# A recurrent layer with a routed expert layer: fixed slots for two chunks instead of one, the upper halves of four chunks moved between engines, and a new set of ranks

## The chip, the cores and the metric

The kernel runs on one core of a Trainium2 chip. The metric is device time in microseconds from the start to the end of one execution; several executions are timed and their median is given. The engines are named as the profile names them: PE (TensorE matmuls) and PEld (its weight loads), DVE (VectorE), ACT (ScalarE), POOL (GpSimd) and SP (SyncE, which here only issues transfers).

## The reference, cut to what matters

```python
# x, r_gate, i_gate: (4, 5056, 256); a_param: (256,)
a_base = 1 / (1 + exp(-a_param))
a_t    = exp(8 * sigmoid(r_gate) * log(clip(a_base)))
x_g    = sqrt(max(1 - a_t * a_t, 1e-6)) * sigmoid(i_gate) * x
h      = a_t[:, t] * h + x_g[:, t]        # a scan over 5056 steps, y[:, t] = h
# the 4 * 5056 = 20224 rows of y go through 8 experts, one for each row
e_idx  = argmax(y @ w_gate)               # the row's expert
gate_w = softmax(y @ w_gate)[e_idx]
eom    = sigmoid(y @ w_output_gate)[e_idx]
out    = gate_w * eom * (relu(y @ w1[e_idx]) @ w2[e_idx])   # w1: 256 x 1024, w2: 1024 x 256
```

## The kernel before, in words

The 20224 tokens are 158 tiles of 128, worked off in 20 chunks of 8 tiles (the last has 6). `chunk(c)` is the front of the kernel. It loads the three inputs in two blocks of 512 tokens, forms the decay and the gated input on ACT and DVE (L570 to L592), scans on DVE (L623), finds a power of two that scales the block (`top`, `norm`, `scale_`), and splits the scaled state into two fp16 parts: `hi`, the upper half (L676 on ACT, or L678, a tensor_scalar on DVE, by the letter of the chunk in `UPPERS`), and `lo`, what is left (L681, DVE). `project` (L702, PE) transposes each tile's two halves and forms the gate logits; `row` (L709, ACT) copies the tile's rows to `rows_all`, and `lz` (L713, DVE) sums the logits. Then come the choice of the expert, the token's rank within it (`ranks`, L743 and L745, PE), its weight and its position, and 8 indirect transfers on POOL (`scatter_rows`, L391) that write the rows of the chunk into the DRAM buffer `xs`, sorted by expert.

The expert weights are loaded in fp32 and split into two fp16 parts that stay in SBUF (`w1r`, `w2r`). `unit(u, ...)` does this for one of 16 matrices (unit 2e is w1 of expert e, unit 2e+1 its w2): a load (L451), a small Gram product on PE that gives a scale (`gram`, L477), then `hi` (L510, ACT) and `lo` (L524, DVE). A unit's fp32 data is staged where the split unit two further on will stand; the last two units, 14 and 15, are staged in the ring `ws`.

Tokens meet their experts in two ways. `slot(s)` takes a number of rows (128 or 256, at the end 64) of one expert, which is only known on the chip: it loads the rows transposed (L1047), copies the expert's w1 from `w1r` to a tile `ws` (two transfers, L1063), multiplies (L1091), takes relu on ACT (L1106) and the lower half on DVE (L1111), multiplies by w2 out of `w2r` (L1137), scales (L1150) and stores rows by an indirect transfer (L1153). `turn(c, e)` is a fixed slot: expert e's first 128 tokens of chunk c have 128 rows of their own in `xs`, so that the expert is known when the program is written and w1 and w2 are read where they lie, with no `ws` copy (L908, L930, L946, L973 or L980, L994, L997). In the turns of chunk 0 with e under 7, called raw, the second product is done in fp32 with the staged, unsplit w2 (L973); the other turns use the split w2 (L980), and DVE forms the lower half of h (L949). Rows of turns that no token fills come from a filling of zeros (`fill`, L1193). Tokens beyond the 128 of a fixed slot go to the ordinary slots.

Which chunk has how many slots is settled when the program is written. Before: 8 turns in chunk 0; 5 slots of 128 in chunk 1, 8 in chunk 2; then 62 slots of 256, three or four in a chunk and one in chunk 3; at the end 23 slots of 128 and 8 of 64. The last 9 and 4 of these stand behind a branch that is taken only if a token needs them (`SPARE`, `THIN_SPARE`, `unused`).

The order of work on every engine is fixed when the program is written, by `in_order`: a list scheduler with estimated times, in which each piece of work has a rank (`UNIT_RANK`, `CHUNK_RANK`, `ROUND_RANK`, `SLOT_RANK`, `UNIT_LOAD` and others) and the lowest rank among the ready ones goes first. Buffers are rings (`Ring`): a tile waits until the tile n before it is released, and until its predecessor in the ring has begun. A ring's order is the order in which the calls stand in the program, so that the place of the call matters:

```python
scaled += [unit(u, STAGED.get(u)) for u in range(E, 2 * E - 2)]   # units 8 to 13
for e in range(HOLD if ROUNDS else 0):
    turn(0, e)
...                                                              # then units 14 and 15
if c < ROUNDS:
    for e in range(0 if c else HOLD, E):
        turn(c, e)
```

The ring `ps_h` (3 tiles) is shared by the units' Gram products and by the first product of the turns and slots.

Of the kernel before, what the change touches and what calls it, by code (L numbers as in the profile page):

```python
# [25 lines left out]
SIZES = (8, 8)  # L26
WIDTHS = (128,128,128)
MODES = 'SSSSSSSSSSSSSSSS'
ROUNDS = 1
HOLD = 0  # L30
RAW = 7
TURNS = (870,)
RESERVE = {128:500,256:1100}
GROW = 80

SPLITS = {"S": "ACT", "D": "DVE"}
SCALED = {"ACT": 1.02, "DVE": 0.7}
SQUARES = 'AAAAA'
UPPERS = 'AAAAA'
BOUNDS = 'AAAAAAAADDDDDDDDDDDD'  # L40

RT = 2
# [6 lines left out]
LANDING = {"Pool": 2.0, "SP": 0.5}  # L49
ADDRESS = 1.11  # L50
SWITCH = 1.28
LAG = 0.00115
ALONE = (0, 1, 2, 3, 4, 5, 6, 7)
QUICK = -11.74482
ROOT = 872.46984
EARLY = -3356.52202
UNIT_RANK = (14.784, 1.135, 649.126, 1304.642, -3219.631, -118.358, 953.446, -19.714, 619.598, 551.943, 729.966, -184.356, 791.67, 1318.467, -195.084, 200.882)
CHUNK_RANK = (-8.611, 721.162, 1331.441, 1446.348, 941.149, 843.802)
FILL = 154.31313
ROUND_RANK = (-265.341,)  # L60
TURN = 103.07338
SLOT_RANK = (837.564, 517.995, 614.48, 621.619)
LOAD_RANK = 5.18213
STAGED = {14: ('ws', 'ws'), 15: ('ws', 'ws')}
WINDOW, WARM = 3.413, (0.8, 0.35)
UNIT_LOAD = (39.858, 449.082, 537.194, 43.57, -91.278, 168.502, 435.996, 1305.65, 173.591, -125.648, -166.337, -60.891, 955.38, -3351.625, 57.178, 964.301)
CHUNK_LOAD = (7.699, -0.953, -160.403, 959.152, 155.261, -58.702)
TAIL = -3981.4538
TOPS = 2
TABLES = -188.10427  # L70
DEPTH = 3
SLACK = (0.152, 0.728, 0.933, 1.2, 0.778, 0.203)
PACE = 9.85e-05

SPREAD = (2.0, 2.6)

SPARE = 9
THIN = 64
HOMES = ("rt", "it", "xt", "ws", "rt", "it", "xt", "ws", "ws")
THIN_AT = 12  # L80
# [112 lines left out]
def rglru_moe(ctx: ExitStack, tc: tile.TileContext, x, r_gate, i_gate, a_param, wg, wog, w1, w2, out, shape):  # L193
# [26 lines left out]
    for c, (t, n) in enumerate(chunks):  # L220
        pending += n * P
        bound_left += n * P
        if c < ROUNDS:
            pending -= TURNS[c]
            bound_left -= min(P, bound_left)
# [21 lines left out]

    xs = tc.dram_tile([E * REGION + ROUNDS * E * P + VOID, ROW // 2], F32, name="xs")

# [117 lines left out]
    zrow = const.tile([P, ROW], F16, name="zrow")  # L367
    dummy = E * REGION + ROUNDS * E * P
    last_row = dummy + VOID
# [20 lines left out]
    def scatter_rows(pos, rows, c):  # L390
# [3 lines left out]
        ins = op.ins  # L394
        past = [tiles["fill"]] if c < ROUNDS else []
        tc.declare_no_dep(ins, group="xs", keep=past, reason="rows of xs are written once, ahead of the loads that read them")
# [144 lines left out]
    def chunk(c):  # L541
# [66 lines left out]
        for b, nb, m, g0, key, ru, iu, xu, root, inputs, scale in blocks:  # L608
            w = work("ACT", 1.04 * scale, root, squares[b // 4:b // 4 + 1] if c in ALONE else squares, rank + ROOT, "S", uses=[iu])
            w = work("DVE", 0.07 + 1.07 * scale, inputs, [w], rank, uses=[iu, xu])  # L610
# [31 lines left out]
        for b in range(0, nt, 4):  # L642
# [30 lines left out]

            def hi(H=H, halves=halves, s_of=s_of, by=UPPERS[c] if c < len(UPPERS) else "A"):
                if by == "A":
# [10 lines left out]
            pu, pold = rings["ps_t"].new()  # L686
            w = work("PE", 0.15, norm, [w, pold], EARLY + c / 100, uses=[pu, au], slack=SLACK[2 + (c > 3)])
            w = work("DVE", 0.33, scale_, [w] + chain["small"], front, uses=[pu])
            by = "DVE" if c < len(UPPERS) and UPPERS[c] == "D" else "ACT"
            w = work(by, (0.1 + 0.95 * scale, 0.07 + 0.7 * scale)[by == "DVE"], hi, [w], front, uses=[iu, xu])  # L690
            cut = work("DVE", 0.07 + 1.15 * scale, lo, [w], front, uses=[iu, xu])
            for j in range(b, b + nb):
# [21 lines left out]

                w = work("PE", 0.277, project, [cut, pold, gates], EARLY + c / 100, uses=[pu, xu], slack=SLACK[c > 3])
                copied.append(work("ACT", 0.48, row, [w, old], front, uses=[pu, used]))
# [57 lines left out]
        def positions():  # L774
# [5 lines left out]

            if c < ROUNDS:
                nc.vector.scalar_tensor_tensor(beyond, carry, -float(P + c * E * P), fixed, op0=ALU.add, op1=ALU.subtract)
# [10 lines left out]
        def counts():  # L793
            pk = tiles["pk", c]
            held = pk[:, nt * E:(nt + 1) * E]
            if c < ROUNDS:
                nc.vector.tensor_scalar(beyond, held, -float(P), 0.0, op0=ALU.add, op1=ALU.max)
                held = beyond
            nc.vector.tensor_tensor(carry, carry, held, op=ALU.add)

        quick = rank + QUICK
        ch = work("DVE", 0.5, choose, lows, quick)
        ex = work("ACT", 0.42, chances, [ch], quick, "E")
        cn = work("DVE", 0.9, chosen, [ch, ex], quick)
        pu, pold = rings["ps_t"].new()
        pk = work("PE", 0.24, ranks, [cn, pold], EARLY + c / 100, uses=[pu], slack=SLACK[c > 3])
        sm = work("DVE", 0.6, sums, [cn, ex], quick)
# [86 lines left out]
    def turn(c, e):  # L894
# [73 lines left out]
        for f in range(NF):  # L968
# [15 lines left out]

            m = work("PE", 0.44 if raw else 0.327, multiply2, [m, evac[f // 4]] + (loaded if raw else split)[2 * e + 1], rank + LAG + f * PACE, uses=[pu, hus[f // 4][0]], slack=SLACK[4] if f == 0 else 0.0)

# [35 lines left out]
    def slot(s):  # L1022
# [103 lines left out]
        for f in range(NF):  # L1126
# [14 lines left out]

            m = work("PE", 0.327 * q, multiply2, [m, evac[f // per], ready] + (every if f == 0 else []), rank + LAG + f * PACE, uses=[pu, hus[f // 4][0], vuse], slack=SLACK[4 + (c > 3)] if f == 0 else 0.0)
            m.placed = True
# [72 lines left out]
    for h in range(2):  # L1216
# [7 lines left out]
        if h == 0:  # L1224
            scaled += [unit(u, STAGED.get(u)) for u in range(E, 2 * E - 2)]
            for e in range(HOLD if ROUNDS else 0):
                turn(0, e)
# [4 lines left out]
    for c in range(NC):  # L1232
# [3 lines left out]
# [3 lines that stand above are left out]
# [59 lines left out]
```

## Time and profile before

| | |
|---|---|
| median of 3 executions | 1034.86 us (1034.28 to 1034.92) |
| the profiled execution: its own time | 1036.0 us |
| its span, first to last instruction | 1034.3 us |
| PE, ACT, DVE, POOL busy, share of the span | 93%, 70%, 66%, 35% |
| mean granted TensorE clock, share of full speed | 0.975 |
| moved by DMA | 245.28 MB |

A busy PE is one with a matmul under way; matmuls overlap, so the mean duration of one is longer than the step from one to the next. The idle time in a row of a group is that of the engine just before the group's instructions.

### The profile page before, as it was taken

To read this page: it belongs to the slowest core of one execution; us is meant where nothing else is said; L and a number is where in the kernel's file an instruction comes from. 1 tells how busy PE (TensorE), PEld (TensorE's weight loads), DVE (VectorE), ACT (ScalarE), POOL (GpSimd) and SP (SyncE) were. 2 spreads that over 40 slices of the span, in tenths; PEclk is the share of its full clock that TensorE was granted. 3 is DMA by queue.
4 is the path that set the end of the run, shared out by engine and by line. 5 is a ranking of instruction groups with operands and counts; after the bars stand their busy time and mean duration, and the time that the engine had idled before them with its cause. 6 is when DMAs were issued, how large, how long until landed. Compare 5 with 4: busy or idle time off the path is not lost.

```text
span 1034.3 us, 29541 instructions
## 1 busy us (share of the span) xinstructions
PE 966.7 (93%) x9884; PEld 869.0 (84%) x9884; DVE 686.4 (66%) x1696; ACT 719.7 (70%) x1149; POOL 360.8 (35%) x346
## 2 busy tenths in 40 slices
PE   3567989889999999999999999999999999999997
PEld 2557978778889888889998999999899888899986
DVE  6696786787777776767677686777867676232231
ACT  8889889989897858677685867768577653232232
POOL 0032361543435342524324243443424234422111
PEclk9857999999999999999999999999999999999999
DMA  9995659998898879777786968778686749636871
GB/s 327 378 362 153 176 167 309 289 317 263 240 267 239 268 213 262 216 231 237 225 241 226 270 228 230 247 210 265 220 250 220 224 155 304 200 115 222 262 226 30
DMA packets 196862, 245.28 MB, mean 237 GB/s; under 512 B 119262, under 2 KB 130527, under 8 KB 196720
## 3 DMA queue, kind: packets, MB, share of 16 engines
q1 hardware_dynamic: 180992, 200.18, 65.3%
q0 software_dynamic: 15728, 43.17, 12.7%
q8 instruction: 94, 1.54, 0.6%
q14 instruction: 48, 0.39, 0.1%
HBM read 79.09 MB, written 45.97 MB: 121 GB/s over the span
## 4 chain that ended last, share of the span: by engine, by line
PE 60%; issue 10%; ACT 10%; DMA 8%; DVE 6%; SPq 3%; POOL 3%; POOLq 0%; ACTq 0%; DVEq 0%
PE po L1137 27%; PE ph L1091 26%; PE pt L702 3%; DMA w2r<-in_moe_w_dram 2%; POOL out_dram L1153 2%; ACT rows_all L709 2%; DVE it L623 2%; PE ph_t L930 1%; DMA ws<-w1r 1%; PE po_t L973 1%; ACT h L1106 1%; DMA it<-in_i_gate_dram 1%; SPq L451 1%; DMA w1r<-in_moe_w_dram 1%; ACT rt L580 1%
## 5 line engine op out<-in xcount | busy, mean ns | idle before, releaser
L1137 PE MATMUL po<-w2r,h 128*128 x3720 | 501.8, 272 | 4.2 <-ACT ot L1150 2.7
L1091 PE MATMUL ph<-xt,ws 128*128 128x256 f16 (+2 forms) x4464 | 494.9, 254 | 7.3 <-DMA ws<-w1r 7.0
L1091 PEld LDWEIGHTS <-ws 128*128 128x128 f16 x4464 | 379.7, 98 | 45.1 <-DMA ws<-w1r 8.7
L1137 PEld LDWEIGHTS <-h 128*128 128x128 f16 x3720 | 355.2, 98 | 48.2 <-issue 5.3
L1106 ACT ACTIVATE h<-ph 128x512 f16<-128x512 f32 (+1 forms) x310 | 182.0, 590 | 229.3 <-PE ph L1091 222.7
L1111 DVE SCALAR_TENSOR_TENSOR h<-ph,h 128x512 f16<-128x512 f32 (+1 forms) x310 | 209.0, 679 | 170.3 <-ACT h L1106 169.3
L1153 POOL DMA_INDIRECT out_dram<-ot,mt x155 | 161.7, 1043 | 399.9 <-ACT ot L1150 365.1
L391 POOL DMA_INDIRECT xs<-rows_all,posi x158 | 178.2, 1128 | 235.9 <-issue 102.7
L709 ACT ACTIVATE rows_all<-pt 128x512 f16<-128x512 f32 x158 | 91.4, 595 | 9.8 <-PE pt L702 5.1
L623 DVE TENSOR_TENSOR_SCAN it<-rt,last,it 128x512 f32<-128x512 f32 (+4 forms) x78 | 96.2, 1241 | 0.3
L1150 ACT ACTIVATE ot<-po,osc 128x256 f32<-128x256 f32 (+1 forms) x155 | 67.5, 472 | 30.5 <-PE po L1137 23.0
L702 PE MATMUL pt<-iw,xt 128*128 128x160 f16 x632 | 71.7, 241 | 13.0 <-ACT xt L676 4.2
L713 DVE TENSOR_REDUCE lz<-pt 128x16 f32<-128x64 f32 x158 | 34.4, 222 | 62.8 <-PE pt L702 37.4
L702 PEld LDWEIGHTS <-xt 128*128 128x128 f16 x632 | 54.2, 102 | 19.3 <-issue 7.1
L592 DVE SCALAR_TENSOR_TENSOR it<-it,xt 128x1024 f32<-128x1024 f32 (+1 forms) x40 | 48.2, 1206 | 29.2 <-ACT it L589 29.2
L580 ACT ACTIVATE rt<-rt,lam 128x512 f32<-128x512 f32 (+1 forms) x80 | 62.0, 812 | 0.2
L681 DVE SCALAR_TENSOR_TENSOR xt<-it,sc,xt 128x1024 f16<-128x1024 f32 (+1 forms) x40 | 50.7, 1267 | 17.2 <-ACT xt L676 17.2
L676 ACT ACTIVATE xt<-it,sc 128x1024 f16<-128x1024 f32 (+1 forms) x40 | 45.6, 1141 | 6.3 <-DVE sc L302 5.1
L576 DVE SCALAR_TENSOR_TENSOR xt<-it,xt 128x1024 f32<-128x1024 f32 (+1 forms) x40 | 48.2, 1205 | 2.5 <-DMA xt<-in_x_dram 1.5
L584 ACT ACTIVATE it<-rt 128x1024 f32<-128x1024 f32 (+1 forms) x40 | 41.8, 1044 | 6.3 <-DVE xt L576 5.8
L589 ACT ACTIVATE it<-it,quarter 128x1024 f32<-128x1024 f32 (+1 forms) x40 | 45.4, 1135 | 0.4
L570 ACT ACTIVATE rt<-rt 128x1024 f32<-128x1024 f32 (+1 forms) x40 | 42.0, 1050 | 3.7 <-DMA rt<-in_r_gate_dram 3.5
(159 smaller groups left out, 702.6 us busy)
## 6 DMA issues: line engine op xcount, KB each, us to landing
ws<-w1r SPq DMA_DIRECT2D x186, 512.0 KB
rt<-in_r_gate_dram SPq DMA_DIRECT2D x39, 512.0 KB
it<-in_i_gate_dram SPq DMA_DIRECT2D x39, 512.0 KB
xt<-in_x_dram SPq DMA_DIRECT2D x39, 512.0 KB
w1r<-in_moe_w_dram SPq DMA_DIRECT2D x7, 1024.0 KB
w2r<-in_moe_w_dram SPq DMA_DIRECT2D x7, 1024.0 KB
xs<-rows_all,posi POOLq DMA_INDIRECT x158, 4.0
out_dram<-ot,mt POOLq DMA_INDIRECT x155, 3.9
```

The source lines that it names most:

```text
L391: op = nc.gpsimd.indirect_dma_start(out=xs[:, :], out_offset=bass.IndirectOffsetOnAxis(ap=pos, axis=0), in_=rows.bitcast(F32), in_offset=None,
L580: nc.scalar.activation(r[:, h], r[:, h], AF.Exp, scale=lam[:, h:h + 1], bias=lam[:, h:h + 1])
L623: nc.vector.tensor_tensor_scan(H[:, h, lo:hi], A[:, h, lo:hi], H[:, h, lo:hi], first, op0=ALU.mult, op1=ALU.add)
L681: nc.vector.scalar_tensor_tensor(halves()[:, 1], H(), s_of(), halves()[:, 0], op0=ALU.mult, op1=ALU.subtract)
L702: nc.tensor.matmul(pt[:, k, h * P:h * P + PIECE], lhsT=halves()[:, k, h, (j % 4) * P:(j % 4 + 1) * P], rhs=iw[:, h, :], start=h == 0, stop ...
L709: nc.scalar.activation(rows_all[:, row_at[j], 0:META].rearrange("p (k h d) -> p k h d", k=2, h=ND), src, AF.Copy)
L1091: nc.tensor.matmul(ph[:, i], lhsT=ws[:, f // 2 % 2, a, c, f % 2 * P:(f % 2 + 1) * P], rhs=xt[:, b * ND + c, 0:w], start=k == 0, stop=k == ...
L1106: newest["relu"] = nc.scalar.activation(part(0, f0), tiles["ph", s, f0], AF.Relu).ins
L1111: nc.vector.scalar_tensor_tensor(part(1, f0), tiles["ph", s, f0], 0.0, part(0, f0), op0=ALU.max, op1=ALU.subtract)
L1137: nc.tensor.matmul(po[:, j], lhsT=hh[:, a, f % 4, j * P:j * P + P], rhs=w2r[:, bass.ds(eo + (b * NF + f) * D, D)], start=f + j + a + b == ...
L1150: nc.scalar.activation(ot[0:pw], tiles["po", s][0:pw, j], AF.Copy, scale=tiles["osc", s][0:pw, j, :])
L1153: op = nc.gpsimd.indirect_dma_start(out=out[:, :], out_offset=bass.IndirectOffsetOnAxis(ap=tiles["mt", s][0:pw, j, 1:2].bitcast(I32), axis=0),
```

## The change

Chunk 1 gets eight fixed slots as chunk 0 has them (`ROUNDS` 2; `TURNS`, the number of tokens that are expected to find room in them), with 1024 more rows in `xs`, which the filling covers as well. By the same rules the slots of 128 become none in chunk 1 and 6 in chunk 2; there are still 62 of 256 (one more in chunks 6 and 9, one less in 7 and 10), and at the end 29 of 128 and 8 of 64, of which the last 15 and 4 stand behind the branch. The fixed slots of chunk 1 are not raw. The turns of experts 0 and 1 of chunk 0 are called ahead of units 14 and 15 (`HOLD` 2), which puts them ahead in the rings. The upper halves of chunks 1 to 4 are formed by DVE (L678) instead of ACT (L676). All ranks and the slacks of the scheduler are new.

```diff
-ROUNDS = 1
-HOLD = 0
+ROUNDS = 2
+HOLD = 2
 RAW = 7
-TURNS = (870,)
+TURNS = (870,870)
...
-UPPERS = 'AAAAA'
+UPPERS = 'ADDDD'
...
-LAG = 0.00115
+LAG = 0.00106
...
-QUICK = -11.74482
-ROOT = 872.46984
-EARLY = -3356.52202
-UNIT_RANK = (14.784, 1.135, 649.126, 1304.642, -3219.631, -118.358, 953.446, ...
-CHUNK_RANK = (-8.611, 721.162, 1331.441, 1446.348, 941.149, 843.802)
-FILL = 154.31313
-ROUND_RANK = (-265.341,)
-TURN = 103.07338
+QUICK = 117.35396
+ROOT = 217.25543
+EARLY = -1051.66239
+UNIT_RANK = (-84.779, 27.039, 146.56, 431.971, 155.352, -58.55, -84.794, ...
+CHUNK_RANK = (-235.93, -111.945, 140.773, 290.077, 20.451, -24.26)
+FILL = 23.029
+ROUND_RANK = (-383.116, -583.193)
+TURN = 5.93459
...
-SPARE = 9
+SPARE = 15
```

Likewise new are `SLOT_RANK`, `LOAD_RANK`, `UNIT_LOAD`, `CHUNK_LOAD`, `TAIL`, `TABLES`, `SLACK` and `PACE`.

## Rows read from the trace of the kernel before

**Rows 1.** The page: busy time by engine, and the span in 40 slices.
```profile
PE 966.7 (93%) x9884; PEld 869.0 (84%) x9884; DVE 686.4 (66%) x1696; ACT 719.7 (70%) x1149; POOL 360.8 (35%) x346
...
PE   3567989889999999999999999999999999999997
...
ACT  8889889989897858677685867768577653232232
```
**Rows 2.** Busy time by stretch: us, PE, PEld, DVE, ACT, POOL, PEclk, DMA share, GB/s.
```profile
0.00:75.00 75.00, 38.93 (x322) 34.69 (x323) 57.56 (x152) 63.77 (x100) 11.30 (x25) 0.80 1.04 363
75.00:90.00 15.00, 7.17 (x58) 6.18 (x56) 9.23 (x27) 14.94 (x23) 0.00 (x0) 0.61 0.75 184
90.00:290.00 200.00, 184.84 (x2095) 166.29 (x2092) 150.28 (x358) 181.41 (x270) 80.90 (x67) 0.99 0.84 243
290.00:1000.00 710.00, 707.89 (x7054) 636.92 (x7052) 461.77 (x1145) 451.16 (x744) 261.94 (x248) 1.00 0.77 232
1000.00:1034.30 34.30, 27.82 (x367) 24.93 (x364) 7.52 (x17) 8.38 (x16) 6.62 (x7) 0.95 0.26 69
```
**Rows 3.** The chain of work that ended last: start, us, what.
```profile
290.60 1.31 PE po L1137 x12
```
**Rows 4.** Waits of PE from 90 to 290 us: total us, times, longest.
```profile
PE ph L1091 <- DMA ws<-w1r: 7.0, 8, 1.9
PE po_t L980 <- ACT ot_t L994: 3.8, 1, 3.8
```
**Rows 5.** Timeline of PE: start, us, what.
```profile
87.50 1.91 PE L477 MATMUL pg<-fw 128*128 128x128 bf16 x16
89.21 3.72 PE L930 MATMUL ph_t<-xt_t,w1r 128*128 128x128 f16 x36
...
951.48 1.17 PE L1091 MATMUL ph<-xt,ws 128*128 128x128 f16 x18
...
956.91 1.17 PE L1091 MATMUL ph<-xt,ws 128*128 128x128 f16 x18
```
**Rows 6.** Busy time by stretch again, two stretches.
```profile
72.00:89.20 17.20, 9.06 (x70) 8.07 (x71) 11.75 (x30) 16.75 (x25) 0.00 (x0) 0.60 0.86 211
...
152.00:290.00 138.00, 127.40 (x1487) 114.48 (x1485) 100.67 (x252) 125.81 (x193) 51.66 (x45) 1.00 0.98 284
```
**Rows 7.** Timelines of POOL and SP: the last scatter of a chunk, its first fetch.
```profile
62.73 0.96 POOL L391 DMA_INDIRECT xs<-rows_all,posi  x1 [0.30 <-issue]
...
68.79 2.27 SPq L908 DMA_TRANSPOSE xt_t<-xs  x1
...
277.44 0.96 POOL L391 DMA_INDIRECT xs<-rows_all,posi  x1 [1.05 <-ACT h L1106]
...
286.13 1.33 SPq L1047 DMA_TRANSPOSE xt<-xs  x1
```
**Rows 8.** Groups of ACT from 90 to 290 us: busy us, mean ns, idle before.
```profile
L1106 ACT ACTIVATE h<-ph 128x512 f16<-128x512 f32 x45 | 26.1, 594 | 2.9 <-PE ph L1091 2.8
...
L589 ACT ACT_TABLE_LOAD x9 | 11.5, 1283 | 0.2
L676 ACT ACTIVATE xt<-it,sc 128x1024 f16<-128x1024 f32 x10 | 11.4, 1145 | 1.7 <-DVE sc L302 1.7
...
L1150 ACT ACTIVATE ot<-po,osc 128x256 f32<-128x256 f32 x19 | 8.6, 469 | 0.5 <-PE po L1137 0.5
```
**Rows 9.** Groups of DVE by shape: busy us, mean ns, idle before.
```profile
L660 DVE TENSOR_REDUCE am<-it 128x1 f32<-128x1024 f32 x23 | 27.8, 1211 | 0.0
...
L383 DVE MEMSET zrow<- 128x264 uint32 x1 | 0.3, 278 | 0.0
```
**Rows 10.** Transfers by line: count, size of one; and the group of the slots' stores.
```profile
ws<-w1r SPq DMA_DIRECT2D x186, 512.0 KB
...
xs<-zrow SPq DMA_DIRECT2D x1, 1056.0 KB
...
L1153 POOL DMA_INDIRECT out_dram<-ot,mt x155 | 161.7, 1043 | 399.9 <-ACT ot L1150 365.1
```

More of the change, by code (lines that the diff above doesn't have):

```diff
@@ L51 @@
 SWITCH = 1.28
-LAG = 0.00115
+LAG = 0.00106
 ALONE = (0, 1, 2, 3, 4, 5, 6, 7)
-QUICK = -11.74482
-ROOT = 872.46984
-EARLY = -3356.52202
-UNIT_RANK = (14.784, 1.135, 649.126, 1304.642, -3219.631, -118.358, 953.446, -19.714, 619.598, 551.943, 729.966, -184.356, 791.67, 1318.467, -195.084, 200.882)
-CHUNK_RANK = (-8.611, 721.162, 1331.441, 1446.348, 941.149, 843.802)
-FILL = 154.31313
-ROUND_RANK = (-265.341,)
-TURN = 103.07338
-SLOT_RANK = (837.564, 517.995, 614.48, 621.619)
-LOAD_RANK = 5.18213
+QUICK = 117.35396
+ROOT = 217.25543
+EARLY = -1051.66239
+UNIT_RANK = (-84.779, 27.039, 146.56, 431.971, 155.352, -58.55, -84.794, 14.651, -43.617, 17.787, -235.287, 145.715, 4.342, -0.395, -798.819, -0.903)
+CHUNK_RANK = (-235.93, -111.945, 140.773, 290.077, 20.451, -24.26)
+FILL = 23.029
+ROUND_RANK = (-383.116, -583.193)
+TURN = 5.93459
+SLOT_RANK = (103.546, 160.443, -183.654, -48.334)
+LOAD_RANK = 39.7946
 STAGED = {14: ('ws', 'ws'), 15: ('ws', 'ws')}
 WINDOW, WARM = 3.413, (0.8, 0.35)
-UNIT_LOAD = (39.858, 449.082, 537.194, 43.57, -91.278, 168.502, 435.996, 1305.65, 173.591, -125.648, -166.337, -60.891, 955.38, -3351.625, 57.178, 964.301)
-CHUNK_LOAD = (7.699, -0.953, -160.403, 959.152, 155.261, -58.702)
-TAIL = -3981.4538
+UNIT_LOAD = (343.79, 237.254, 197.318, 198.135, 397.366, -101.845, -43.231, 105.079, 197.907, 8.526, -185.281, 225.229, 97.674, -117.131, 398.254, 205.512)
+CHUNK_LOAD = (101.047, 25.577, 4.303, 1.54, -185.995, -16.184)
+TAIL = -950.62491
 TOPS = 2
-TABLES = -188.10427
+TABLES = 453.62907
 DEPTH = 3
-SLACK = (0.152, 0.728, 0.933, 1.2, 0.778, 0.203)
-PACE = 9.85e-05
+SLACK = (0.455, 0.656, 0.555, 1.414, 0.584, 0.178)
+PACE = 9.03e-05
 SPREAD = (2.0, 2.6)
-SPARE = 9
+SPARE = 15
 THIN = 64
```

## The prediction

> **What bounds the kernel now.** I read the page first. PE is busy 93% of the span, but the slices say where the missing 7% lie: PE's digits are 3 to 9 in the first nine slices of 25.9 us and 9 from there to the last but one, while ACT stands at 8 or 9 through the first twelve slices and mostly at 5 to 8 after them [rows 1]. So the kernel has two regimes. The table by stretch puts numbers on them: PE is idle 36.1 us of the first 75, 7.8 us of the next 15, 15.2 us from 90 to 290, 2.1 us in the 710 us after that, and 6.5 us in the last 34 [rows 2]. The sum is 67.6 us, the 1034.3 us of the span less PE's 966.7. The chain of waits says the same in another way: by 290 us it is, and from there on stays, an almost unbroken sequence of PE's two products, 12 matmuls in 1.31 us [rows 3]. From there on the end is fixed by how much matmul work is left. What can be won is idle PE time ahead of 290 us, less any work that is added to PE.
>
> Ahead of 290 us three things meet. To 75 us the transfers are full (share 1.04 of 16 engines, 363 GB/s): 16 weight matrices and the inputs of two chunks [rows 2]. From 75 to 90 us PE waits for the front. From 90 to 290 us ACT is busy 181.4 of 200 us, DVE 150.3, and the transfers of the second part of it are full again, 0.98 from 152 to 290 us [rows 2, 6]. Chunk 5, the first whose slots find PE saturated, shows that the front sets the pace: its last scatter starts at 277.4 us and its first fetch at 286.1 us, as soon as the scatter has landed [rows 7].
>
> **The change, part by part.**
>
> *One more slot's work on PE.* Eight fixed slots are added and seven slots of 128 go (13 become 6). The 62 slots of 256 stay. At the end 23 less 9 and 29 less 15 are both 14 slots of 128 ahead of the branch, and 4 of 64. Before, the stores of the slots are 155 [rows 10]: 62 times 2, 13, 14 and 4, so the branch was not taken. Whether it is taken after, I counted from the reference's own inputs: the fixed slots take 871 tokens of chunk 0 and would take 892 of chunk 1, and what is left at the end needs 14 slots of 128 and 4 of 64 with either kernel. So the end of the kernel is the same work. A split fixed slot and a slot of 128 have the same 72 matmuls; two neighbouring slots at the end stand 956.91 - 951.48 = 5.4 us apart [rows 5]. PE gets 5.4 us more.
>
> *Fewer weight copies.* Seven slots bring two copies of 512 KB each [rows 10]: 7.3 MB, which at 284 GB/s is 26 us of transfers in a stretch of 138 us that is full [rows 6]. PE's waits for `ws` from 90 to 290 us are 7.0 us [rows 4]. The bounds are nothing and 7.0; I take 5.0, because over half of the slots of 128 no longer ask for a copy and the others find the queues emptier. The inputs on the same queue come earlier too. SP issues 14 copies less, and the eight new fetches stand in for seven old ones, so nothing is queued longer on SP.
>
> *The filling.* It doubles, 1056 KB more [rows 10]; at 363 GB/s [rows 2] that is 3.0 us in a stretch in which the weights are waited for. Bounds nothing and 3.0; I take half, 1.5, since after the change two turns can run before the last weights are needed. The scatters of chunk 1 now wait for the filling too; it is landed long before.
>
> *Two turns ahead of units 14 and 15.* Turn 0 starts on PE at 89.2 us, right behind unit 15's Gram product at 87.5 us [rows 5]. Its rows were there much sooner: chunk 0's last scatter is at 62.7 us and the fetch at 68.8 us [rows 7]. What held it is the ring `ps_h`, in which it stands behind unit 15. With `HOLD` 2, turns 0 and 1 can run from about 72 us. From 72 to 89.2 us PE is idle 17.2 - 9.1 = 8.1 us, and ACT only 0.4 [rows 6]. So the bounds are nothing and 8.1; I take 4.0, because the granted clock there is 0.60, near the lower of its two levels (1.2 of 2.4 GHz), and because the relus of the turns must find room on ACT. Behind the turns on PE now stand the Gram products of units 14 and 15, and behind those the last splits; they are needed by turn 7 alone among the turns of chunk 0, and then by the slots, which now begin eight turns later. This is the cover for a delay of units 14 and 15; without it a turn's time, some 6 us, would be paid once.
>
> *Upper halves on DVE.* Two blocks in each of four chunks: 8 x 1.145 = 9.2 us leave ACT [rows 8]. The extra slot's two relus and one scaling add 2 x 0.594 + 0.469 = 1.7 us [rows 8], so ACT has 7.5 us less of its 181.4. On DVE no tensor_scalar of this size is in the trace. The nearest row in size with one large input is the reduction over 1024 elements, 1.21 us, and from below a memset of 264 words, 0.28 us [rows 9]. I take 1.21, the nearer in size: 9.7 us, against 49.7 us of idle DVE from 90 to 290 us [rows 2], which hide it. Were DVE full, it would cost what ACT gains. The Trainium skill (VectorE: DVE Perf Modes, The perf-mode tier table) gives 1227 ns for an fp32 tensor_scalar of 2048 elements in SBUF; half of that is an estimate of 0.61 us for ours, DVE's part would be 4.9 us, and no run here shows it yet. What this is worth to PE: of its 15.2 idle us from 90 to 290 us, 7.0 are waits for `ws` and 3.8 the one wait of turn 7's second product [rows 4]; 4.4 are left, spread over waits for the front. Bounds nothing and 4.4; I take 3.5. The wait of 3.8 us I leave as it is, since turn 7 still wants the last split.
>
> *The ranks.* They can shift anything. A measure of what they may do on ACT is the table loads: 9 of 1.28 us stand ahead of square roots from 90 to 290 us [rows 8], for 11 blocks, where one in a chunk would be 6. Each such load has another on the way back, so 3 fewer pairs would save 7.7 us of ACT, and as many more would cost it. I take nothing.
>
> *Sum.* Won on PE: 5.0 + 4.0 + 3.5 = 12.5 us. Paid: 5.4 + 1.5 = 6.9 us. The profiled execution would go from 1036.0 us (1034.3 us of span and 1.7 around it) to 1030.4 us, and the median of the runs, which is 1.1 us under the profiled one, from 1034.9 to 1029.3 us. ACT's account gives a like size: with 7.5 us less work, chunk 5 is scattered up to 7.5 us sooner.
>
> **The rivals.**
>
> *A: the forecast*, 1022 to 1032 us.
>
> *B: PE's early idle time is used up.* The turns fill all 8.1 us from 72 to 89.2 us and all 15.2 us go from 90 to 290 us: 23.3 - 5.4 = 17.9 us won, 1017 us; with part of the 36.1 us before 75 us it is 1013. For it speaks that chunk 0 can now be worth routing sooner, as its turns no longer wait for unit 15; against it, that ACT is full in just these stretches.
>
> *C: nothing moves.* The front stays at its pace because something other than ACT holds it (the inputs' loads, DVE with its longer list), the extra slot goes into idle time, and the end is within 2 us of now. Against it speaks ACT's 91% from 90 to 290 us.
>
> *D: slower.* PE has no room for the extra slot. This is the mechanism: from 90 us on PE is busy 92%, and if the turns of chunk 1 stand in line behind chunk 0's while the front does not come sooner, the 5.4 us go straight to the end, with up to 3.0 for the filling: 1040 to 1043 us. It decides from the point at which less than 5.4 us of the idle 23.3 are recovered. Ranks that move a load or a unit to the wrong place end here as well. The Trainium skill (Perfetto Trace Analysis, Identifying the Most-Contended Engine) says to relieve the engine with the highest occupancy; read over the whole span that is PE, ACT's 9.2 us would be worth nothing, and case D follows. The rows by stretch agree with it after 290 us and not before.
>
> *E: the branch is taken* because the count comes out otherwise on the chip: 15 slots of 128 at 5.4 us and 4 smaller ones, about 100 us.
>
> **How the numbers follow.** A 0.40, B 0.18, C 0.12, D 0.28, E 0.02. The likeliest is A, 1029.3 us, by itself 1022 to 1032. The range for 8 in 10 goes from B's 1013 us to D's 1043 us; outside lie E, some of D's worse ranks and little of B. 0.2% of the time is 2.1 us, about what a measurement can tell from no change. Faster by more than that: A and B, 0.58; within it: C, 0.12; slower: D and E, 0.30.
>
> **What would show it.** Stores of the slots: 148 instead of 155, and 16 of turns. Turn 0 starting on PE near 72 us instead of 89.2. `ws` copies 172 instead of 186, and PE's wait for them under 3 us. L678 x8 on DVE, and ACT's L676 at 32. The last scatter of chunk 5 at 268 to 273 us, and PE's idle time ahead of 290 us down from 59.1 to some 47 us. The forecast is wrong if that scatter does not come sooner, if PE's early idle time does not fall by 5.4 us, or if a new wait stands ahead of turn 7 or of the first slots.

## The result and the profile after

The changed kernel takes 1041.3 us (median of 5 executions, 1038.81 to 1042.7) against 1034.86 us: ratio 1.0053, 95% interval 1.0039 to 1.0067. It is slower by 6.4 us, and the forecast was 1029.3 us. The profiled execution, the longest of the five, took 1042.7 us, of which 1041.0 us are span.

Work moved as the diff says. The page of the changed kernel, its totals and two of its rows of slices:

```profile
PE 969.4 (93%) x9956; PEld 873.1 (84%) x9956; DVE 693.7 (67%) x1711; ACT 711.7 (68%) x1146; POOL 368.3 (35%) x347
...
PE   2467899998999999999999999999999999999997
...
ACT  7889999787996877777777778768755223222222
```

PE has 72 matmuls more, one slot's [rows 1]. There are 148 stores of slots and 16 of turns, 172 `ws` copies instead of 186, and no sign of the branch. The table by stretch, with the same columns as before [rows 2, 6]:

```profile
0.00:75.00 75.00, 32.60 (x279) 29.68 (x279) 52.98 (x145) 62.85 (x90) 12.41 (x25) 0.75 1.03 361
75.00:90.00 15.00, 11.79 (x125) 10.80 (x126) 11.21 (x33) 14.04 (x29) 0.00 (x0) 0.77 0.97 253
90.00:290.00 200.00, 184.85 (x2099) 166.02 (x2098) 157.54 (x365) 180.73 (x271) 81.21 (x68) 0.97 0.74 207
290.00:1000.00 710.00, 705.71 (x7000) 635.35 (x6998) 462.28 (x1150) 443.58 (x739) 267.00 (x247) 1.00 0.76 228
```
```profile
72.00:89.20 17.20, 13.65 (x149) 12.36 (x148) 13.57 (x37) 16.21 (x30) 0.00 (x0) 0.75 0.99 281
152.00:290.00 138.00, 129.68 (x1511) 116.34 (x1509) 100.55 (x252) 119.76 (x187) 49.81 (x45) 0.99 0.83 231
```

From 90 to 290 us PE is idle 15.2 us, to a tenth what it was. (That it is the same to a tenth is chance: in the profile of a second run of the changed kernel it is 12.8 us.) ACT, which was to be relieved by 7.5 us, is busy 180.7 us instead of 181.4. Part of the reason stands in its groups: the upper halves (L676) fall from 11.4 to 4.6 us in this stretch, but the splits of the weights (L510) rise from 14.2 to 17.6 us, since splits that fell before 90 us now come after it. In the changed kernel:

```profile
L676 ACT ACTIVATE xt<-it,sc 128x1024 f16<-128x1024 f32 x4 | 4.6, 1140 | 0.2 <-DVE sc L302 0.2
...
L510 ACT ACTIVATE w1r<-fw,wsc 128x1024 f16<-128x1024 f32 x2 | 2.2, 1138 | 0.0
```

From 72 to 89.2 us PE's idle time did fall from 8.1 to 3.6 us, and the transfers from 152 to 290 us have room (0.83 instead of 0.98). PE's waits from 90 to 290 us, and the upper halves on DVE:

```profile
PE ph L1091 <- DMA ws<-w1r: 3.0, 2, 2.7
PE norm L296 <- ACT xt L662: 2.6, 2, 1.6
PE pt L702 <- DVE xt L678: 2.3, 1, 2.3
...
PE po_t L980 <- ACT ot_t L994: 1.2, 1, 1.2
```
```profile
L678 DVE TENSOR_SCALAR xt<-it,sc 128x1024 f16<-128x1024 f32 x8 | 6.4, 801 | 0.6
```

The waits for `ws` shrank from 7.0 to 3.0 us, and the wait of 3.8 us ahead of turn 7's second product is gone [rows 4]; the 1.2 us at L980 are a turn of chunk 1, at 188.5 us. New waits for the front stand beside them. PE's timeline shows what became of the two early turns (start, us, what, idle time before it):

```profile
80.94 1.91 PE L477 MATMUL pg<-w1r 128*128 128x128 bf16 x16
82.65 1.65 PE L477 MATMUL pg<-w2r 128*128 128x128 bf16 x16
...
85.05 3.17 PE L930 MATMUL ph_t<-xt_t,w1r 128*128 128x128 f16 x54
...
93.67 1.08 PE L477 MATMUL pg<-fw 128*128 128x128 bf16 x16
...
97.57 3.70 PE L973 MATMUL po_t<-w2r,h_t 128*128 128x256 f32 x16
102.91 0.38 PE L296 MATMUL norm<-am,ones 128*128 128x1 f32 x2 [1.64 <-ACT xt L662]
105.56 0.45 PE L702 MATMUL pt<-iw,xt 128*128 128x160 f16 x2 [2.27 <-DVE xt L678]
106.88 0.98 PE L702 MATMUL pt<-iw,xt 128*128 128x160 f16 x6 [0.87 <-DVE xt L681]
107.66 1.91 PE L477 MATMUL pg<-fw 128*128 128x128 bf16 x16
...
110.09 0.85 PE L930 MATMUL ph_t<-xt_t,w1r 128*128 128x128 f16 x6
```

Turn 0 starts at 85.05 us, 4.2 us earlier, not at 72: Gram products of other units and chunk 1's `pt` still stand ahead of it on PE. Unit 14's Gram product is at 93.67 us and unit 15's at 107.66 us (87.5 before [rows 5]). Behind it stands turn 2, at 110.09 us. In the kernel before turn 2 is part of these 72 matmuls, its first half at about 97.40 + 48 x 0.055 = 100 us:

```profile
97.40 4.18 PE L930 MATMUL ph_t<-xt_t,w1r 128*128 128x128 f16 x72
```

So turns 0 and 1 come sooner and turn 2 comes 10 us later; in between PE waits for the front (and from 105 to 110 us works at a granted clock of 0.50), which is at chunk 2 by then: these are chunk 2's first `norm` and `pt` (chunk 1's `pt` are the second 32 of the trace, from 64.4 to 80.8 us). The last scatter of chunk 5:

```profile
277.55 0.96 POOL L391 DMA_INDIRECT xs<-rows_all,posi  x1 [0.30 <-ACT rows_all L709]
```

It is not sooner at all [rows 7]. The front's lead is real earlier on: the last scatters of chunks 2, 3 and 4 start at 147.4, 200.9 and 233.0 us, against 151.6, 203.5 and 238.8 us. Then it is gone. The rows show part of where it goes. Of PE's waits for `ws` the longest grew from 1.9 to 2.7 us; it ends at 236.7 us, and the granted clock falls right behind it. The table by stretch, first of the kernel before, then of the changed kernel:

```profile
145.70:149.00 3.30, 3.30 (x22) 2.32 (x22) 3.30 (x4) 3.01 (x4) 2.69 (x3) 0.71 0.80 297
...
225.00:250.00 25.00, 23.32 (x249) 20.33 (x247) 16.91 (x38) 24.06 (x36) 11.09 (x10) 1.00 0.94 288
```
```profile
225.00:250.00 25.00, 21.10 (x227) 18.52 (x225) 13.71 (x36) 19.70 (x31) 8.76 (x8) 0.93 1.01 293
...
234.00:236.70 2.70, 0.04 (x1) 0.00 (x0) 0.22 (x1) 2.70 (x5) 0.00 (x0) 1.00 1.05 407
236.70:240.00 3.30, 3.29 (x30) 2.90 (x31) 1.38 (x2) 0.88 (x2) 0.00 (x0) 0.61 1.03 407
240.00:243.00 3.00, 2.82 (x26) 2.46 (x25) 1.72 (x8) 2.92 (x6) 1.00 (x1) 0.85 0.63 156
```

PE has stood idle for 2.7 us when the clock drops to 0.61, near the lower of its two levels; by 243 us it is at 1.00 again. My estimate of the price from these rows is 3.3 x 0.39 + 3.0 x 0.15 = 1.7 us on top of the wait. The transfers have room on average from 152 to 290 us (0.83), but not here (1.05). In the kernel before such a fall, to 0.71, stands behind turn 7's wait of 3.8 us; its waits for `ws` are eight, none over 1.9 us, and from 152 to 290 us its clock stays at 1.00 [rows 4, 6].

PE's idle time does not say all, because short gaps count as busy. So I also count matmuls: each kind times its step at full speed (0.109 us for one of 256 columns: six lie 0.656 us apart; 0.0545 for 128; 0.068 for 160; 0.219 for one in fp32). What the clock shows less this sum is PE's lost time. At 300 us it is 88.8 us after and 89.5 us before. A slightly different count, at the end of this text, has 91.0 for the same 89.5, so that 0.7 is within what such a count can tell: of the 11.0 us that the change was to win net of the filling, next to nothing is left. Until then PE has 5.4 us more to do, and from 290 to 1000 us it idles 2.2 us more. 5.4 - 0.7 + 2.2 = 6.9, near the span's 6.7. This is bookkeeping: it says where the time stands, not what would bring it back.

### The profile page after: what moved, and what is told of

Read it like the earlier page. It is cut to its first block, busy times and chain, and to the rows that moved or that the text cites. A ratio compares the mean times of both kernels' runs of the same rounds, so it can differ in the third digit from the quotient of the medians.

```text
span 1041.0 us, 29527 instructions
## 1 busy us (share of the span) xinstructions
PE 969.4 (93%) x9956; PEld 873.1 (84%) x9956; DVE 693.7 (67%) x1711; ACT 711.7 (68%) x1146; POOL 368.3 (35%) x347
## 4 chain that ended last, share of the span: by engine, by line
PE 72%; ACT 9%; DMA 7%; DVE 6%; issue 3%; SPq 1%; POOL 0%; POOLq 0%; ACTq 0%; DVEq 0%
PE po L1137 33%; PE ph L1091 31%; PE pt L702 3%; DVE it L623 2%; DMA ws<-w1r 2%; PE ph_t L930 2%; PE po_t L973 1%; DMA w2r<-in_moe_w_dram 1%; DMA it<-in_i_gate_dram 1%; DMA rt<-in_r_gate_dram 1%; ACT w1r L510 1%; ACT L589 1%; ACT rows_all L709 1%; ACT it L589 1%; DVE it L592 1%
## 5 line engine op out<-in xcount | busy, mean ns | idle before, releaser
L1137 PE MATMUL po<-w2r,h 128*128 x3552 | 479.6, 273 | 4.1 <-ACT ot L1150 2.1
L1091 PE MATMUL ph<-xt,ws 128*128 128x256 f16 (+2 forms) x4128 | 469.6, 257 | 5.3 <-DMA ws<-w1r 4.1
L1091 PEld LDWEIGHTS <-ws 128*128 128x128 f16 x4128 | 358.7, 98 | 41.9 <-DMA ws<-w1r 5.3
L1137 PEld LDWEIGHTS <-h 128*128 128x128 f16 x3552 | 340.9, 98 | 46.9 <-issue 6.2
L1111 DVE SCALAR_TENSOR_TENSOR h<-ph,h 128x512 f16<-128x512 f32 (+1 forms) x296 | 199.8, 678 | 193.2 <-ACT h L1106 191.3
L1106 ACT ACTIVATE h<-ph 128x512 f16<-128x512 f32 (+1 forms) x296 | 173.7, 589 | 175.7 <-PE ph L1091 174.8
L1150 ACT ACTIVATE ot<-po,osc 128x256 f32<-128x256 f32 (+1 forms) x148 | 64.1, 468 | 90.9 <-PE po L1137 80.3
L930 PE MATMUL ph_t<-xt_t,w1r 128*128 128x128 f16 x768 | 48.8, 220 | 1.1 <-DVE h_t L949 1.1
L930 PEld LDWEIGHTS <-w1r 128*128 128x128 f16 x768 | 45.7, 99 | 2.4 <-issue 1.4
L573 ACT ACTIVATE it<-it 128x1024 f32<-128x1024 f32 (+1 forms) x40 | 41.9, 1048 | 8.2 <-DMA it<-in_i_gate_dram 8.1
```

The costliest lines, as they stand in the source:

```text
L930: nc.tensor.matmul(tiles["ph", s, f0][:, i], lhsT=w1r[:, o:o + P], rhs=tiles["xt16", s][:, b * ND + d, 0:P], start=k == 0, stop=k == 3 * N ...
L1091: nc.tensor.matmul(ph[:, i], lhsT=ws[:, f // 2 % 2, a, c, f % 2 * P:(f % 2 + 1) * P], rhs=xt[:, b * ND + c, 0:w], start=k == 0, stop=k == ...
L1106: newest["relu"] = nc.scalar.activation(part(0, f0), tiles["ph", s, f0], AF.Relu).ins
L1111: nc.vector.scalar_tensor_tensor(part(1, f0), tiles["ph", s, f0], 0.0, part(0, f0), op0=ALU.max, op1=ALU.subtract)
L1137: nc.tensor.matmul(po[:, j], lhsT=hh[:, a, f % 4, j * P:j * P + P], rhs=w2r[:, bass.ds(eo + (b * NF + f) * D, D)], start=f + j + a + b == ...
L1150: nc.scalar.activation(ot[0:pw], tiles["po", s][0:pw, j], AF.Copy, scale=tiles["osc", s][0:pw, j, :])
```

## The experiments

My theory after the result: the gains exist, but the place of units 14 and 15 and the ranks take them back. One rival: ranks are fitted to one structure, and nothing can be told by planning again. The other, which came up on the way: the front and PE are matched, so that what PE wins while the front runs becomes a wait for the front. Where an experiment changes a part without planning again, the order of all other work stays as in its base kernel.

The jobs ran on several chips, of two kinds. On two of them the kernel before took 1034.9 and 1034.4 us; on the second of these the changed kernel was run again, at 1042.9 us and a ratio of 1.0072 (1.0052 to 1.0093). On three others the kernel before itself takes 1049.6 to 1052.2 us, and there, on the one of the three where it ran, the changed kernel is level: 0.999 (0.9971 to 1.0009). No chip had two of these jobs, so that a chip and its job can't be told apart. Ratios are therefore compared within one kind of chip only, called first and second kind below; across jobs of the second kind they rest on that one control.

**Units 14 and 15 out of the turns' ring, and `HOLD` 0; both planned again.** (First kind.)

```diff
-        pg, old = rings["ps_h"].new()
+        own = "ps_t" if u in STAGED else "ps_h"     # units 14 and 15; the tile alike
+        pg, old = rings[own].new()
```
```diff
-HOLD = 2
+HOLD = 0
```

> The changed kernel, but the Gram products of units 14 and 15 take their tile from another ring, so that they no longer stand in line with the turns; the order of work is planned anew. Theory RING (the two turns put ahead push unit 15 back, and turn 2 stands behind unit 15): unit 15's Gram product well before 107 us, turn 2 on PE at about 101 us instead of 110, time 1034 to 1037 us. Rival FILLING (the larger filling delays all weight loads) and rival SUM (the extra slot's 5.4 us cannot be won back): 1040 to 1042 us as before the edit.

> The changed kernel with HOLD 0: no turn ahead of units 14 and 15; planned anew. RING: turn 0 starts later than 85 us, but turns 2 to 7 come sooner, time 1035 to 1039 us. Rival, the forecast's own step (two early turns win 4 us): 1044 to 1046 us. SUM: 1041 us.

Ratios 1.0419 (1.0397 to 1.0441) and 1.0303 (1.0276 to 1.033). Two small edits of the structure cost 39 and 25 us against the changed kernel, with the same ranks. I put that down to the ranks; no ranks were fitted to either edit, so the times say nothing about the edits alone. The trace of the first says something about the theory, though. Its turns are no longer held up: turn 0 starts at 80.6 us, turn 2 at about 90. PE from 75 to 125 us, changed kernel and this run, with the stretch behind:

```profile
75.00:125.00 50.00, 39.96 (x408) 35.72 (x409) 42.82 (x95) 48.92 (x79) 13.46 (x11) 0.86 0.68 186
125.00:200.00 75.00, 71.66 (x896) 66.17 (x895) 61.85 (x140) 67.47 (x101) 34.76 (x27) 1.00 0.62 163
```
```profile
75.00:125.00 50.00, 45.91 (x531) 42.49 (x530) 24.99 (x38) 29.66 (x42) 4.67 (x4) 0.96 0.30 64
125.00:200.00 75.00, 53.73 (x542) 45.87 (x543) 57.33 (x136) 62.20 (x92) 25.42 (x24) 0.80 0.61 168
```

PE does 123 matmuls more by 125 us, while ACT is busy 59% and DVE 50% of the stretch: chunk 1's `norm` has its place behind these turns, at 121.1 us instead of 58.9, and chunk 1's last scatter comes at 158.3 us instead of 108.0. PE then idles 21 of 75 us. Here the turns that came early at the front's cost won nothing.

**The ranks exchanged.** The new ranks and slacks on the structure before, and the old ones on the changed structure. (First kind.)

```diff
-UNIT_RANK = (14.784, 1.135, ...      # kernel before: and all others alike
+UNIT_RANK = (-84.779, 27.039, ...
```

> The kernel before with the new ranks and slacks alone (one round of turns, HOLD 0, upper halves on ACT). If the new ranks were the part that costs: 1.005 or more to the kernel before by a few us, 1040 us on a chip that takes 1035. Theory FIT (a set of ranks fits one structure only): 15 us or more slower, 1050 to 1075. If the ranks matter little: within 3 us.

> The changed kernel with the old ranks and slacks (the second round of turns gets the rank of chunk 1's slots before). FIT: 15 us or more slower than the kernel before, 1050 to 1080 us on a chip that takes 1035. If the structure is what costs and the ranks are not: 1035 to 1045.

1.0198 (1.0172 to 1.0224) and 1.0736 (1.0709 to 1.0763). Either set is bad on the other structure, by 20 and 76 us against the kernel before. (The old set has no rank for a second round of turns; the second figure rests on the one that I put there.) The prediction took nothing for the ranks; an ill-fitting set costs more than all its other terms together, so that they can't be costed apart from the structure.

**The upper halves, order kept.** In the changed kernel back on ACT (first kind), in the kernel before on DVE (second kind).

```diff
-            def hi(..., by=UPPERS[c] if c < len(UPPERS) else "A"):
+            def hi(..., by="A"):     # kernel before: by="D" if 1 <= c <= 4 else "A"
```

> The changed kernel with the upper halves of chunks 1 to 4 formed by ACT again, everything else and the planned order the same: ACT gets 9.2 us back ahead of 290 us. Theory FRONT (ACT sets the pace there, as forecast): 1046 to 1050 us. Rival (PE's order of turns sets it, ACT has slack): 1040 to 1043 us.

> The kernel before with one part of the change alone: the upper halves of chunks 1 to 4 on DVE, the planned order of all other work as it was. FRONT (ACT sets PE's pace ahead of 290 us): 1026 to 1031 us, as putting them back on ACT cost the changed kernel 9 us. Rival (the gain exists only with the new order, or DVE's longer list gives it back): 1033 to 1037 us.

Back on ACT: 1050.3 us, 1.0143 (1.0124 to 1.0162), 9.0 us more than the changed kernel's 1041.3 and 7.4 more than the 1042.9 us of its second run, against 9.2 us of ACT's time that come back. Chunk 5's last scatter comes at 283.9 us instead of 277.6. In the kernel before, 1.0006 (0.9992 to 1.002): ACT is busy 169.3 us from 90 to 290 us, where two near copies of that kernel on the same kind of chip have 175.7 and 178.0, and nothing comes of it. So undoing the move costs most of its ACT time in the order that was planned for it, and making it brings nothing in the order that was planned without it. The two were measured on different kinds of chip, so that a part of the difference may be the chip's.

**The fillings, order kept.** Chunk 1's filling and the filling of the unused rows issued behind unit 13's load (changed kernel, first kind); the unused rows' alone (kernel before, second kind, twice).

```diff
-            xs[E * REGION:dummy].rearrange("(k p) d -> p k d", p=P),
+            xs[E * REGION:E * REGION + E * P].rearrange("(k p) d -> p k d", p=P),
...
+                if u == LATE_AT:     # 13: the rest, and the unused rows
+                    hooks[0]()
```

> The changed kernel, with chunk 1's part of the filling and the filling of the void issued right behind unit 13's load instead of at 11 us; the planned order of PE, ACT and DVE is the same. FILLING: SP is held 4 to 8 us less, units' Gram products come 4 us or more sooner, time 1036 to 1038 us. RING and SUM: 1040 to 1042 us, since turn 2 still stands behind unit 15 and the filling was not what delayed that unit's staging.

> The kernel before with the filling of the void issued behind unit 13's load instead of at 12.6 us, planned order as it was. FILLING (early filling delays the weights and these the end): 1031 to 1033 us. Rival (the front's ACT work hides it): 1034 to 1036 us.

> The kernel before with its second filling (the 1320 KB for rows that no chunk writes) issued on SP behind unit 13's load, instead of ahead of the loads that PE's first Gram products wait for; all else the same. On another chip this came out 0.2% shorter. If SP's 4.15 us at that transfer hold back the weights, 1032 to 1033.5 us against 1034.4; if they are hidden, 1034 to 1035.

1.005 (1.0032 to 1.0069), so 1039.6 us, between the two forecasts: 1.7 us under the first run of the changed kernel and 3.3 under the second, hardly more than its executions scatter. Unit 15's Gram product is some 4 us earlier, as theory FILLING had it; little of that reaches the end. In the kernel before it is 0.9981 (0.9965 to 0.9996) and, on another chip, 0.9994 (0.9982 to 1.0006). SP does stand longer at these transfers:

```profile
12.18 8.73 SPq L1202 DMA_DIRECT2D xs<-zrow  x1
```

8.73 us, where the same transfer holds it 4.15 us in the kernel before. By these runs both fillings together cost the changed kernel some 2 to 3 us, within the noise of such a comparison. Of the versions that do the whole computation, none came out faster than the kernel before in a way that held when it was repeated.

**Unit 15 or turn 2 moved by hand, order kept otherwise.** First units 14 and 15's chain pulled ahead, then turn 2's products and relus pulled ahead of unit 15's Gram product. (Second kind.)

```diff
+        move(marked["first", 0, 2], marked["second", 0, 1])
+        move(marked["relu", 0, 2], [marked["result", 0, 1]])
+        move(marked["second", 0, 2][:4], marked["relu", 0, 2] + between[:1])   # norm
+        move(marked["second", 0, 2][4:], marked["second", 0, 2][:4] + between) # norm, pt, pt
```

> The changed kernel with its planned order, save that units 14 and 15 are moved by hand: unit 14's Gram product ahead of turn 0 on PE, its split behind unit 12's, unit 15's last load behind that, unit 15's Gram product behind turn 1, and turn 2's first product behind it. RING (the 6.6 us that PE loses from 100 to 125 us against the kernel before are the two units' line behind the turns, and reach the end): turn 2 on PE at 101 to 104 us instead of 110, time 1035 to 1038 us. Rival (the loss is made good by 200 us anyway, the front sets the pace): 1040 to 1042 us.

> The changed kernel with its planned order kept, but for one turn: turn 2's first product stands on PE directly behind turn 1's second, its second product before and behind unit 12's neighbours of chunk 1 and ahead of unit 15's Gram product, instead of behind that; its two relus move with it. PE idled there from 101 to 110 us. Theory HOLD (the place of units 14 and 15 ahead of turn 2 is what took back the gain of the two early turns): PE's lost time at 125 us falls by 4 to 6 us and the time with it, 1036 to 1038 us against 1041.3. Rival PACE (what PE wins ahead of chunk 5 turns into idle time, because the slots' rows come when the front gives them): the lost time at 125 us falls the same, but at 300 us by under 2 us, and the time by 0 to 2 us, 1039 to 1041. Under 0.2% in both directions counts for PACE.

The first, 1.0089 (1.0062 to 1.0116), did not do what it was for: unit 15's load came 2.4 us sooner and its Gram product at 110.4 us, since unit 14's now held up turn 0. The second did what it was for and came out at 1.0089 (1.0069 to 1.0109), some 10 us worse than the control's 0.999 (on another chip of that kind). PE's timeline of it:

```profile
102.49 2.69 PE L936 MATMUL ph_t<-xt_t,w1r 128*128 128x128 f16 x40
105.67 0.61 PE L936 MATMUL ph_t<-xt_t,w1r 128*128 128x128 f16 x8 [0.49 <-issue]
106.11 0.33 PE L296 MATMUL norm<-am,ones 128*128 128x1 f32 x2
107.16 1.99 PE L982 MATMUL po_t<-w2r,h_t 128*128 128x256 f32 x8 [0.72 <-ACT h_t L952]
111.12 0.31 PE L707 MATMUL pt<-iw,xt 128*128 128x160 f16 x2 [1.97 <-DVE xt L683]
```

Turn 2 fills the gap from 102.5 us on, and the two small matmuls of `norm`, from which the scale of chunk 2's first block comes, now wait behind it: 106.1 instead of 102.8 us in the control. Of these 3.3 us 1.4 were there before the moved work, as turn 0 itself starts at 85.8 instead of 84.4 us. Chunk 2's first `pt` slips from 105.5 to 111.1 us, ACT waits 1.9 and 2.4 us ahead of the turn's relus, and PE's lost time at 125 us is 80.9 instead of 74.9 us. So this gap was not free for PE to fill: what stands in it is the front's latency, `norm`, scale, upper half, lower half, `pt`. The run moves the turn's relus on ACT as well, so that it does not tell PE's share from ACT's. Unit 15's place alone is not the cause that I first took it for.

**The same 13.9 us of matmuls left out at four places.** One of the three products is left out, in both matmul groups, in eight turns of chunk 1 (192 matmuls), in the seven slots of chunks 2 and 3 (176), in four slots of 256 of chunk 12 (128), or in the last four of 256 (128); the rows concerned are less exact. Each is 13.9 us of PE at full speed.

```diff
-                        for a, b in ((0, 0), (0, 1), (1, 0)):
+                        for a, b in TERMS[cut(s)]:     # ((0, 0), (1, 0)) where cut
```

> The changed kernel, planned order as it was; the eight turns of chunk 1 leave out one of the three products of halves, the upper half times the lower half of the weights, in both layers: 192 matmuls less, 13.9 us of PE from about 145 to 205 us by the step of 0.054 us for 128 columns and 0.109 us for 256. SUM (PE has no room, its work goes straight to the end): 1027 to 1030 us. FRONT (PE waits for the front anyway, the work fits into idle time): 1037 to 1041 us.

> The changed kernel as it is, timed in the same chip job as the next one, as the last job's chip took 1052 us for the kernel before: its ratio to the kernel before should be 1.004 to 1.007, as first measured, if the slower chip slows both alike.

> The changed kernel with one of three products of halves left out in chunk 1's turns (192 matmuls, 13.9 us of PE), again, now beside the changed kernel itself. SUM (their work goes straight to the end): 12 to 15 us under the changed kernel. FRONT (PE waits there anyway): 0 to 4 us under it. In between: part of it is hidden, and the difference says how much.

> The changed kernel with one of the three products (upper half of the weights by lower half of the rows, and its like in the second product) left out in the six slots of 128 of chunk 2 and the one slot of 256 of chunk 3, so that the outputs of these rows are less exact: 176 matmuls, 6 x 1.74 + 3.49 = 13.9 us of PE at full speed, the same as in the eight turns of chunk 1 (there 3.7 us of it reached the end). Theory PACE (work ahead of chunk 5 is partly free): 3 to 8 us shorter, 1033 to 1038. Rival (PE is the bound from 90 us on, so a microsecond of work is a microsecond of time): 13 to 14 us, 1027 to 1028.

> As the run with seven slots, but with the product left out in four slots of 256 of chunk 12, in the stretch in which PE is saturated: 128 matmuls, 4 x 3.49 = 13.9 us. Every theory expects it to reach the end whole: 12 to 14 us shorter, 1027 to 1029. If less comes, PE is not the bound there either and the whole account by PE's idle time is in doubt.

> The product left out in the last four slots of 256 (13.9 us of matmuls, as in the runs before), which PE works off at about 890 to 935 us, behind the last matmul of the front at 794 us. The run with chunk 12's four slots gave back less than was expected: PE idled there 7.2 us from 600 to 650 us, mostly for rows that DVE and ACT had not split yet. Theory PACE, widened (as long as the front runs, PE's work and the front's are matched, and work taken from PE turns into waits for the front): here, with the front done, 12 to 14 us reach the end against the control of the same job. Rival (something else holds the order throughout): 8 us or less.

> The changed kernel itself as a control on the same chip: ratio to the kernel before 1.005 to 1.007 by both theories. If its ratio is nearer to 1, the loss depends on the chip.

| left out in | PE works it off at | kernel | its control | of 13.9 us reach the end |
|---|---|---|---|---|
| turns of chunk 1, first kind | 145 to 205 us | 1039.19 us | 1042.9 us, same job | 3.7 |
| turns of chunk 1, second kind | 145 to 205 us | 0.9994 | 0.999 | none |
| slots of chunks 2 and 3 | 200 to 255 us | 0.9971 | 0.999 | 2 |
| four slots of chunk 12 | about 600 us | 0.9972 | 0.999 | 2 |
| last four slots of 256 | 890 to 935 us | 1035.6 us | 1047.89 us, same job | 12.3 |

A figure with a ratio in its row rests on a control from another job; the intervals are about 0.2% to either side, so that the 3.7 and the two 2 are not told from nothing, and the 12.3 is clear. I had expected 12 to 14 us of chunk 12's slots, by every theory, and got 2. Here is where it went: the table by stretch, first of the control, then of the kernel with the cut, and what PE waits for in the latter from 600 to 650 us.

```profile
550.00:600.00 50.00, 49.21 (x474) 43.96 (x472) 36.58 (x89) 39.13 (x62) 19.09 (x18) 1.00 0.89 244
600.00:650.00 50.00, 50.00 (x487) 45.16 (x486) 38.96 (x106) 39.95 (x65) 19.19 (x17) 1.00 0.87 246
```
```profile
550.00:600.00 50.00, 47.63 (x455) 42.23 (x453) 35.20 (x88) 38.15 (x62) 19.99 (x19) 1.00 0.89 249
600.00:650.00 50.00, 42.81 (x400) 36.03 (x400) 39.54 (x103) 40.84 (x68) 19.55 (x18) 1.00 0.91 256
```
```profile
PE pt L703 <- DVE xt L682: 2.7, 2, 1.6
PE pt L703 <- ACT xt L677: 2.1, 2, 1.4
PE po L1141 <- ACT h L1110: 0.9, 1, 0.9
PE norm L297 <- DVE am L661: 0.9, 1, 0.9
```

PE, at 100% from 600 to 650 us in the control, now idles 7.2 us of the 50, mostly for rows that DVE and ACT have not split yet, with both of them at 80% and the transfers at 0.91. With the front done (its last matmul is at 793.8 us in the changed kernel), the same 13.9 us reach the end nearly whole. So at the three places that were tried while the front runs, PE and the front are matched within a few microseconds, and at the one behind it PE is the bound nearly alone. All this is the changed kernel with its order kept: ACT and DVE are not full, and whether a new order for a kernel with less work on PE would move the front sooner was not tried.

## Why the prediction was wrong

**The extra slot, 5.4 us:** the work is right, PE's 72 matmuls. That it goes to the end is only bookkeeping: 13.9 us taken out of the very turns of chunk 1 brought 3.7 us on the first kind of chip and nothing on the second.

**Fewer copies, 5.0 us:** right in kind, 4.0 us measured (waits for `ws` 7.0 to 3.0 us, full transfers 0.98 to 0.83). The one long wait that is left brings a fall of the clock with it, some 1.7 us by my estimate, which the sum did not have. Nor did it have the other side: the 3.8 us ahead of turn 7, which I left as they were, went away, and the fall of the clock behind them too.

**The filling, 1.5 us:** not contradicted; the run with both fillings put off is 1.7 to 3.3 us shorter, which is near the noise.

**Two turns ahead, 4.0 us:** the size was right where it was looked for, 4.5 us less idle time from 72 to 89.2 us, though PE is idle 6.3 us more ahead of 75 us (42.4 instead of 36.1), which the sum did not look at. That `ps_h` was what held turn 0 is half of it: put ahead of units 14 and 15 in that ring, turn 0 starts at 85.05 us and not at 72. The first step that failed is the cover, that units 14 and 15 "are needed by turn 7 alone". In the ring `ps_h` and on PE's list turns 2 to 7 stand behind unit 15's Gram product, so that turn 2 starts 10 us later, and PE's lost time grows by 8.4 us from 100 to 125 us, where in the kernel before it grows by 0.3. The prediction's own price for a lost cover was "some 6 us". At 300 us the two counts are level again, so these 8 us do not reach the end as such. And the run with turn 2 pulled ahead shows that the cover's loss is not a mere matter of order: what PE waits for in between is the front of chunk 2.

**Upper halves on DVE, 3.5 us, and chunk 5 "up to 7.5 us sooner":** this step failed. DVE took 0.80 us for each, between the estimate from the Trainium skill's page (0.61) and the row I took (1.21), so DVE's part is 6.4 us and not 9.7. ACT is busy 0.7 us less from 90 to 290 us and not 7.5, and chunk 5 comes at 277.55 us. I had credited the relief against the old kernel, as if the order would stay. The run of the kernel before with this move alone brings nothing; the run with it undone costs 7.4 to 9.0 us, so the new order needs it. It pays for something that the new order loses. The lead, 2.6 to 5.8 us up to chunk 4, goes between chunk 4 and chunk 5, where the rows show the one wait of 2.7 us for `ws` and the fall of the clock behind it. That these alone take the lead is not shown.

**The ranks, nothing:** taken at nothing with no measure that could tell. The two exchanges cost 20 and 76 us. A rank set goes with a structure, and the measure that I used, the table loads ahead of square roots (9 before and 9 after from 90 to 290 us), does not see this.

**What bounds the kernel:** "from there on the end is fixed by how much matmul work is left" is the deeper error, and the step on which the whole sum stands. It read a PE without waits as a PE that alone decides. The runs with a product left out show that 2 of 13.9 us count at 600 us and 12.3 at 900 us. So idle time won ahead of 290 us can't simply be added up to time; the run with the Gram products out of the ring shows the other side, where PE's early work pushed the front back. Which share of the 6.4 us each of these steps has stays open.

**The rivals:** D came, at its own price of 1040 to 1043 us and by its own condition: of the 23.3 us of idle time that it names 4.6 were recovered, less than 5.4 (and of all idle time ahead of 290 us nothing: 42.4 + 3.2 + 15.2 = 60.8 us against 59.1). That the price fits is in part luck. Its mechanism, that the slot's work goes straight to the end, would have brought back nearly all of the 13.9 us that were left out of chunk 1's turns, and 3.7 at most came back; on the second kind of chip the changed kernel is not slower at all. The Trainium skill (Perfetto Trace Analysis, Identifying the Most-Contended Engine) says to optimize the engine with the highest occupancy first; read over the whole span, where PE's weight loads are busy 84% and ACT 70% [rows 1], it would have forecast this sign. But the runs speak against that reading too, since relieving PE itself by 13.9 us at 600 us brought 2.

## What to carry to other kernels

An engine that is busy 100% without waits is not yet the only bound: leave a known amount of its work out at two or three places and see how much of it reaches the end. In an order that a scheduler fixed in advance, a part can cost or bring another amount than in another order, so price it with the order kept, against both kernels, on one chip. And before idle time of an engine is filled, look at what small instruction of the producer's chain stands in that gap: filling one in which two matmuls of `norm` stood made the kernel some 10 us longer, and eight turns ahead of chunk 1's front put that front back by 50 us. Look at the granted clock too when counting waits: here it fell to 0.61 behind one wait of 2.7 us, which cost PE some time more.

## What the runs showed of the chip

The same kernel takes 1034 us on some chips and 1050 to 1052 us on others, and the granted clock does not tell them apart (0.975 in its profile on the first kind, 0.972 to 0.976 in those of its near copies on the second). By the count of matmuls, PE's lost time there goes on growing in the stretch that is saturated, in a run of the kernel before with one filling moved from 96.2 us at 300 us to 106.0 at 900, where on the first kind it goes from 91.0 to 92.5 (a slightly different count than above, the same for both). The changed kernel loses less of it there, 92.1 to 98.0 us; by this count the 8.0 us less at 900 us make good its 5.4 us of extra work, which fits its being level on those chips. What is slower in them I did not find. A comparison of two kernels within 1% holds for the kind of chip on which it was made.
